# A recurrent attention with an MLP on one core: batch 0's attention in whole chunks of 128 tokens

## The chip, the cores and the metric

One core of a Trainium2 chip runs the kernel. It has a matrix engine (PE, with a weight load, PEld, ahead of each product), three engines for elementwise work (DVE, ACT, POOL), and a queue (SP) that mostly starts DMAs; ACT starts some as well. Each engine takes its own queue in order, and waits where an operand isn't ready. PE and the three others work on SBUF; PE's results go to PSUM banks, which DVE and ACT read.

The metric is the device time of one execution in microseconds (us), as the median of several runs. Before the change that is 420.07 us (three runs, 419.74 to 420.17).

## The reference

Four batches, eight heads, 768 tokens, head dimension 48. The attention keeps a 48x48 state for every batch and head, which decays with w and takes in k times v at each token:

```python
for t in range(S):
    kt, vt, rt = (k[:, :, t], v[:, :, t], r[:, :, t])
    cur = np.einsum('bhd,bhe->bhde', u[None] * kt, vt)
    y[:, :, t] = np.einsum('bhd,bhde->bhe', rt, state + cur)
    state = w[None, :, :, None] * state + np.einsum('bhd,bhe->bhde', kt, vt)
```

The heads side by side give x with 384 columns per token. It is mixed along the tokens through rank 32, and then goes through a two-layer MLP:

```python
xt = x.transpose(0, 2, 1)
h = xt @ U @ V
u = x + h.transpose(0, 2, 1)
ch = np.maximum(u @ w_ch1, 0.0) @ w_ch2
return (u + ch).astype(np.float32)
```

The weights U, V, w_ch1 (384x1536) and w_ch2 (1536x384) come as 64-bit floats, the rest as 32-bit.

## The kernel before

**Attention by chunks.** The loop over tokens is unrolled into chunks of C = 128 tokens, NCH = 6 for a batch. With tables of powers of w, r and k of a chunk are scaled so that the products of r with k, masked to earlier tokens (`am`), times v give the part inside the chunk, and r times the state S gives the part of earlier chunks; the token's own term is `dv` (r times k times u, summed over a head to `dg`, times v). In batch 0 a chunk is done in two halves of 64 tokens: 64x64 scores in four quadrants of the array, one state for each half, and two products that need the odd heads of v with the halves of the rows swapped. That swapped copy, `vsw`, is loaded by DMAs of its own (`a_load_odd`). `a_first` begins chunk 0, `a_part(n, 0)` and `a_part(n, 1)` do the two halves of the output of chunk n and the scores and states of chunk n + 1. Between them a one-element copy (`seen`) makes the second half wait for the first. Of the later batches some chunks use the same functions and others `a_chunk`; the change leaves their computation as it is.

**Preparing a chunk** (`prepare`): `a_load` loads r, k and v; `a_ks` multiplies k by a table (`tab`); `a_tr` turns k and r with four transposes each on PE and scales them on the way out of PSUM to `kT` (ACT or DVE) and `rT` (DVE); `a_dv` and `a_dg` make the token's own term.

**From x to the MLP.** `c_gx` sums U's product with each chunk of x in the bank `wake`, `c_g0` makes `Gs` of it, `c_x` turns x on PE into the banks `pu`, `c_xu` adds V's product with Gs there and splits the result in a high and a low part, `uTh` and `uTl`. The MLP (`m_1`, `m_2`) then needs, for each of 12 slices f, the converted weights `w1s` and `w2s`, and takes three products for each block since high and low parts are multiplied apart. Its first product reads `uTh` of batch 0.

**Weights.** A unit is loaded as 64-bit words (`raw_w`), joined to 32-bit floats by steps on ACT and DVE (names `raw_w`), and split into high and low parts (ACT, then DVE or POOL). At most three units are loaded at a time. Units for slice f are called `raw_w_f`; one is of w_ch1 and one of w_ch2, told apart by their shapes in the DMA queue (128x3x256 and 128x768).

**What sets the order.** `Plan` keeps every operation with a key, a due time given by `at(t, ...)`, and a cost in ns. At build time it schedules them on the five queues by these costs and keys, and the instructions are then issued in the order of the planned starts. So queues mix attention, weights and MLP, and a change of a key or a cost moves instructions on all engines. Where PE would stand idle in the front of the program, the planner adds products of the identity with itself (`wake` with `ident`); they compute nothing that is used. Batches 1 to 3 have their attention in between the MLP products of the batch ahead of them.

## Time and profile before

| | us |
|---|---|
| median of three runs | 420.07 |
| the profiled execution | 420.94 |
| its span, first to last instruction | 419.1 |
| PE busy | 408.1 (97%) |
| DVE busy | 263.9 (63%) |
| ACT busy | 134.8 (32%) |
| POOL busy | 74.6 (18%) |

Busy time of PE counts each product from its start to its modelled end, and products overlap: 97% doesn't say that PE is at its peak, and the wake products are in it. The page's chain of work that ended last lies to 91% on PE, 72% on the MLP's products. The page's row of the sixteen DMA engines, in 40 slices of some 10.5 us, shows them busy through the first half:

```profile
DMA  9978969899557677755677814520100510001001
```

### The profile page before, as it was taken

The numbers are of one execution on the slowest core, as the hardware profiler recorded it, in microseconds if no ns is written. First come the engines' busy times: TensorE is split into PE (matmuls) and PEld (weight loads), VectorE is DVE, ScalarE is ACT, GpSimd is POOL, SyncE is SP. The second block draws the span as 40 slices with busy tenths as digits, with TensorE's granted clock in tenths as the row PEclk, the third lists the DMA queues.
The fourth block names the chain that finished last, engine by engine and source line by source line (L and its number), as shares of the span: only waits on it lengthen the run. The fifth ranks groups of instructions, "written<-read, shape, count | busy, mean of one in ns | idle before, by whom it ended". The sixth has DMA issues, their size and how long they took to land.

```text
span 419.1 us, 12257 instructions
## 1 busy us (share of the span) xinstructions
PE 408.1 (97%) x5164; PEld 393.3 (94%) x5164; DVE 263.9 (63%) x594; ACT 134.8 (32%) x358; POOL 74.6 (18%) x114
## 2 busy tenths in 40 slices
PE   8998999999999999999999999999999999999994
PEld 8887999999999898999999999999999999999993
DVE  6878998889898559877784358866523361122122
ACT  2467967547641415212113130112113121111110
POOL 2642150145621103321000003321000000000000
PEclk9999999999999999999999999999999999999998
DMA  9978969899557677755677814520100510001001
GB/s 145 149 160 256 201 163 242 125 224 234 94 85 154 142 144 132 149 103 87 137 140 107 152 68 64 101 39 2 59 2 0 114 57 2 0 2 58 2 0 61
DMA packets 181951, 43.53 MB, mean 104 GB/s; under 512 B 168961, under 2 KB 180354, under 8 KB 181890
## 3 DMA queue, kind: packets, MB, share of 16 engines
q1 hardware_dynamic: 176706, 41.21, 49.1%
q10 hardware_dynamic: 5184, 1.48, 2.0%
q8 instruction: 42, 0.69, 0.7%
q14 instruction: 19, 0.16, 0.1%
HBM read 36.18 MB, written 6.49 MB: 102 GB/s over the span
## 4 chain that ended last, share of the span: by engine, by line
PE 91%; DVE 4%; ACT 2%; issue 1%; POOL 0%; DVEq 0%; ACTq 0%; POOLq 0%
PE p L347 72%; PE wake L347 3%; PE pav L836 3%; PE pav L842 3%; PE pab L795 3%; PE pab L810 2%; PE pu L347 2%; PE ptk L756 1%; PE pG L1040 1%; PE pav L821 1%; DVE am L967 1%; PE ptr L756 1%; ACT dv L725 1%; DVE SW L1004 1%; DVE ut L1136 1%
## 5 line engine op out<-in xcount | busy, mean ns | idle before, releaser
L347 PE MATMUL p<-uTh,w1s 128*128 128x384 f32 x576 | 147.5, 336 | 0.0
L1163 DVE SCALAR_TENSOR_TENSOR hl<-p,hh 128x384 fp32r<-128x384 f32 x96 | 53.2, 555 | 114.9 <-ACT hh L1162 114.5
L347 PE MATMUL p<-w2s,hh 128*128 128x384 f32 x576 | 119.9, 340 | 0.5 <-ACT hh L1162 0.4
L1162 ACT ACTIVATE hh<-p 128x384 fp32r<-128x384 f32 x96 | 47.2, 491 | 222.8 <-PE p L347 220.2
L347 PEld LDWEIGHTS p<-uTh,w1s 128*128 128x128 f32 x576 | 103.2, 188 | 0.5
L347 PEld LDWEIGHTS p<-w2s,hh 128*128 128x128 f32 x576 | 100.0, 188 | 2.4 <-ACT hh L1162 1.1
L347 PE MATMUL p<-uTl,w1s 128*128 128x384 f32 x288 | 96.5, 335 | 0.0
L347 PE MATMUL p<-w2s,hl 128*128 128x384 f32 x288 | 66.1, 335 | 0.0
L347 PEld LDWEIGHTS p<-uTl,w1s 128*128 128x128 f32 x288 | 54.0, 188 | 0.3 <-DVE uTl L1095 0.3
L347 PEld LDWEIGHTS p<-w2s,hl 128*128 128x128 f32 x288 | 51.4, 188 | 0.1
L795 PE MATMUL pab<-rT,kT 48*64 48x64 f32 x768 | 30.6, 223 | 1.8 <-issue 1.0
L836 PE MATMUL pav<-vsw,am 64*64 64x48 f32 x384 | 30.4, 222 | 0.1
L842 PE MATMUL pav<-S,rT 48*64 48x48 f32 x704 | 29.5, 218 | 0.0
L836 PEld LDWEIGHTS pav<-vsw,am 64*64 64x64 f32 x384 | 25.2, 134 | 1.9 <-issue 1.0
L795 PEld LDWEIGHTS pab<-rT,kT 48*64 48x64 f32 x768 | 24.9, 134 | 2.1 <-ACT dv L725 0.8
L842 PEld LDWEIGHTS pav<-S,rT 48*64 48x64 f32 x704 | 25.8, 135 | 0.0
L836 PE MATMUL pav<-ldv,am 64*64 64x48 f32 x320 | 24.2, 221 | 0.0
L705 POOL MEMSET ks<- 128x128 f32 x24 | 4.9, 204 | 101.9 <-PE pav L842 57.0
L967 DVE TENSOR_TENSOR am<-pab,mask 128x256 f32<-128x256 f32 x48 | 19.4, 417 | 5.4 <-PE pab L810 3.9
L836 PEld LDWEIGHTS pav<-ldv,am 64*64 64x64 f32 x320 | 20.2, 134 | 2.5 <-issue 2.1
L810 PE MATMUL pab<-ldv,ks 64*48 64x48 f32 (+1 forms) x576 | 21.1, 212 | 0.0
L995 DVE TENSOR_TENSOR S<-pab,SW 112x192 f32<-112x192 f32 x40 | 14.0, 351 | 8.2 <-PE pab L810 5.5
(136 smaller groups left out, 520.2 us busy)
## 6 DMA issues: line engine op xcount, KB each, us to landing
raw_w<-in_moe_w_ch_dram SPq DMA_DIRECT2D x24, 384.0 KB, 4.7
out_dram<-x SPq DMA_DIRECT2D x21, 192.0 KB, 2.4
ldr<-in_r_dram SPq DMA_DIRECT2D x20, 192.0 KB, 3.1
ldk<-in_k_dram SPq DMA_DIRECT2D x20, 192.0 KB, 3.5
ldv<-in_v_dram SPq DMA_DIRECT2D x20, 192.0 KB, 3.9
bl<-in_r_dram SPq DMA_DIRECT2D x79, 48.0 KB, 2.6
bl<-in_k_dram SPq DMA_DIRECT2D x79, 48.0 KB, 2.4
vsw<-in_v_dram SPq DMA_DIRECT2D x42, 48.0 KB, 2.7
```

The source lines that it names most:

```text
L347: return nc.tensor.matmul(*args, **kw)
L705: op("POOL", 250, lambda: nc.gpsimd.memset(ks.t[:, :, D:], 0.0), [(ks, "pad")], [])
L725: nc.scalar.activation(dv.t[:, h], vt()[:, h], AF.Copy, scale=dg.t[:, h:h + 1])
L756: nc.tensor.transpose(pt.t[:, q * C:(q + 1) * C], src().rearrange("p h d -> p (h d)")[:, q * PE_:(q + 1) * PE_], ident_)
L795: return [lambda q=q, i=i: nc.tensor.matmul(pt.t[(i ^ j) * C2:(i ^ j) * C2 + C2, q * C2:(q + 1) * C2], lhsT=kT.t[rows, q, i * C2:(i + 1) * ...
L810: return nc.tensor.matmul(pt.t[j * HP:j * HP + m, SU + q * D:SU + (q + 1) * D], lhsT=ks.t[half, 2 * q + j, :m], rhs=vt()[half, 2 * q + j, ...
L836: return nc.tensor.matmul(to(q, j, i), lhsT=am[j].t[half, q, :], rhs=vsw[n].t[half, q, :] if j else vt()[half, 2 * q, :], start=((i == 1 i ...
L842: return nc.tensor.matmul(to(q, row, i), lhsT=rT.t[rows, q, i * C2:(i + 1) * C2], rhs=St[n, i].t[rows, q, :], start=False, stop=((alone or ...
L967: on_dve(256, lambda e: e.tensor_tensor(am.t, abs_[n][j].t[:, :SU].rearrange("p (h t) -> p h t", h=NP), mask_.unsqueeze(1).broadcast_to([1 ...
L995: on_dve(192, lambda e, new=new, ptv=ptv, dec=decayed[n, j]: e.tensor_tensor(new.t, ptv(), dec.t, ALU.add), [new], [pt, decayed[n, j]])
L1162: on_act(384, lambda: nc.scalar.activation(hh.t, pt.t[:, :TB], AF.Relu), [hh], [pt])
L1163: on_dve(384, lambda e: e.scalar_tensor_tensor(hl.t, pt.t[:, :TB], 0.0, f32(hh.t), ALU.max, ALU.subtract), [hl], [pt, hh])
```

## The change

Batch 0 gets functions of its own. A chunk is now taken whole: `f_scores` makes 128x128 scores, heads of even number in the upper half of the array's rows and odd ones in the lower (head dimension 48 on 64 rows each), and masks them with a 128x128 mask `before`; `f_state` makes one state for each chunk with full 128-row products; `f_out` makes the part inside the chunk (`inner`, all 128 rows) and that of the state (`outer`, the two row halves), into two banks, one for even and one for odd heads, and adds dv in two halves of 192 columns. No swapped copy of v is loaded for batch 0, and `seen` goes from it.

The powers of w come from doubling (`powers`): w is loaded as four rows of 112 and turned on PE, then each of seven products on DVE doubles the number of powers, up to 128; a reversed copy of them, turned on PE, is the table `tabf` for batch 0. The tables of the later batches are made from the same powers further down (`tables`, `turn_table`). ks is on POOL from chunk 2 on, dv on POOL for all chunks of batch 0, and the zeroing of pads moves from DVE to POOL.

U is kept once instead of three times, and batch 0 sums its product with x in four groups of 32 columns (`g_sum`), in the way of the later batches; `c_g` replaces `c_g0`, so Gs comes by four copies to `gf` and three steps on it.

Keys and costs of the planner change: batch 0's chunks are due every 4.5 instead of 5.5, the MLP's begin at 42 instead of 46. The planner now starts engines at times of their own, holds back a ready operation for a more urgent one that is about to be ready, and adds a wake product only where more of a gap is left.

```diff
+    KS = 2
+    NQA = 3
...
-    tabT = cbuf([PD, 2, NP, C2 + 2], F32, "tabT")
+    tabT = cbuf([PD, NP, C2], F32, "tabT")
     wi = cbuf([PD, NP, 1], F32, "wi")
     wm = cbuf([PD, NP, 1], F32, "wm")
+    wif = cbuf([PD, NP, 1], F32, "wif")
+    wmf = cbuf([PD, NP, 1], F32, "wmf")
...
-    Uf = cbuf([128, NCH, 3, R], F32, "Uf")
+    Uf = cbuf([128, NCH, 1, R], F32, "Uf")
...
+    pw = big([PD, NP, C + 2], F32, "pw")
+    tabf = big([128, DM], F32, "tabf")
...
+    def powers():
+        p = pw.t
+        op("POOL", 112, lambda: nc.gpsimd.memset(p[:, :, 0:1], 1.0), [(pw, 0)], [])
+        pt0 = bank("tr", "pt_w")
+        pe(120, lambda: nc.tensor.transpose(pt0.t[:PD, :NP], wq.t, ident_[:NP, :NP]), [pt0], [wq])
+        on_dve(4, lambda e: e.tensor_scalar(p[:, :, 1:2], pt0.t[:PD, :NP].unsqueeze(2), W_LO, W_HI, ALU.max, ALU.min),
+               [(pw, 1)], [pt0])
+        m = 1
+        while m < C:
+            on_dve(4 * m, lambda e, m=m: e.tensor_mul(p[:, :, m + 1:2 * m + 1], p[:, :, 1:m + 1],
+                                                      p[:, :, m:m + 1].broadcast_to([PD, NP, m])), [(pw, 1)], [])
+            m *= 2
+        back = xbuf([PD, NP, C], F32, "hh", NH, "back")
+        on_dve(512, lambda e: e.tensor_copy(back.t, p[:, :, C - 1::-1]), [back], [pw])
+        turn_table(back, tabf, "tabf")
+        on_dve(4, lambda e: e.reciprocal(wif.t, p[:, :, C:C + 1]), [wif], [pw])
+        on_dve(4, lambda e: e.tensor_copy(wmf.t, p[:, :, C:C + 1]), [wmf], [pw])
...
-        if n < 4 or not front(n):
+        if not front(n):
...
+                  kb + [tabf if front(n) else tab],
+                  only="DVE" if n < KS else "POOL" if front(n) else None)
...
+        if i == 0 and front(n):
+            on_dve(512, lambda e: e.tensor_tensor(xT.t[:PD], by_pair(), pw.t[:, :, :C], ALU.mult), [xT], [pt, pw])
+            return
...
+    def f_scores(n):
+        rT, kT = trs[n]
+        abs_[n] = [bank(t, f"pab_{n}_{j}") for j, t in enumerate(AB)]
+        def product(q, j):
+            rows = head_rows(j)
+            return nc.tensor.matmul(abs_[n][j].t[:, q * C:(q + 1) * C], lhsT=kT.t[rows, q, :], rhs=rT.t[rows, q, :],
+                                    start=True, stop=True)
+        pe(950, lambda: in_turn(*([lambda q=q, j=j: product(q, j) for q in range(NP)] for j in range(2))), abs_[n], [rT, kT],
+           tiled=True)
+        ams[n] = []
+        for j in range(2):
+            am = xbuf([128, NP, C], F32, "bl", 5, f"am_{n}_{j}")
+            ams[n].append(am)
+            on_dve(512, lambda e, am=am, j=j: e.tensor_tensor(am.t, abs_[n][j].t.rearrange("p (q t) -> p q t", q=NP),
+                                                              before_.unsqueeze(1).broadcast_to([128, NP, C]), ALU.mult),
...
+        def product(q, j):
+            m = D if j else HP
+            return nc.tensor.matmul(pt.t[j * HP:j * HP + m, q * D:(q + 1) * D], lhsT=ks.t[:, 2 * q + j, :m],
+                                    rhs=vt()[:, 2 * q + j, :], start=True, stop=True)
+        pe(480, lambda: in_turn(*([lambda q=q, j=j: product(q, j) for q in range(NP)] for j in range(2))), [pt], [ks, *vb],
+           tiled=True)
...
+    def f_out(n):
+        vt, vb = vs[n]
+        rT = trs[n][0]
+        avp[n] = [bank(t, f"pav_{n}_{j}") for j, t in enumerate(("av", "mm"))]
+        def inner(q, j, i):
+            return nc.tensor.matmul(avp[n][j].t[i * C2:(i + 1) * C2, q * D:(q + 1) * D],
+                                    lhsT=ams[n][j].t[:, q, i * C2:(i + 1) * C2], rhs=vt()[:, 2 * q + j, :],
+                                    start=(q == 0), stop=(not n and q == NP - 1), skip_group_check=True)
+        def outer(q, j):
+            rows = head_rows(j)
+            return nc.tensor.matmul(avp[n][j].t[:, q * D:(q + 1) * D], lhsT=rT.t[rows, q, :], rhs=St[n, 0].t[rows, q, :],
+                                    start=False, stop=(q == NP - 1), skip_group_check=True)
+        for j in range(2):
+            pe(500, lambda j=j: in_turn(*([lambda q=q, i=i: inner(q, j, i) for q in range(NP)] for i in range(2))),
+               [avp[n][j]], [ams[n][j], *vb], tiled=True)
+        if n:
+            pe(950, lambda: in_turn(*([lambda q=q, j=j: outer(q, j) for q in range(NP)] for j in range(2))), avp[n], [rT, St[n, 0]],
+               tiled=True)
+        x = xs[n] = xbuf([128, DM], F32, "x", NX, f"x_{n}")
...
+    def g_sum(pt, c0, ns):
+        w4 = DM // 4
+        for n in ns:
+            for g in range(4):
+                nc.tensor.matmul(pt.t[g * R:(g + 1) * R, c0:c0 + w4], lhsT=Uf.t[:, n % NCH, 0],
+                                 rhs=xs[n].t[:, g * w4:(g + 1) * w4],
+                                 start=(c0 == 0 and n % NCH == 0), stop=(n % NCH == NCH - 1), skip_group_check=True)
+    def c_gx(*ns):
+        return pe(170 * len(ns), lambda: g_sum(wk, 128, ns), [(wk, "g")], [Uf] + [xs[n] for n in ns], tiled=True)
...
-    T0, PER = 46.0, 1.95
+    T0, PER = 42.0, 1.85
+    UV, GX, UVC = -84.9, (3, 33.0), (30.0, 33.0)
     EARLY, LEAD = 4, 12.0
-    FRONT, EACH = 9.0, 5.5
+    FRONT, EACH = 9.0, 4.5
+    UB = -88.5
+    SC, SU_, TABLES = 2.0, 0.0, 30.0
...
+        for i, f in enumerate([fs[j] for j in (2, 0, 1, 3)] if front(n) else fs):
...
+            if front(n):
+                at(t - SC, lambda n=n: f_scores(n))
+                at(t - SU_, lambda n=n: f_state(n))
+                at(t, lambda n=n: f_out(n))
+                at(t - 0.1, lambda n=n: a_dg(n))
+                if c >= GX[0]:
+                    at(max(t + per - 0.05, GX[1] + 0.1 * c), lambda n=n: gx.append(c_gx(*(range(n + 1) if n == GX[0] else [n]))))
+                continue
```

**PE, inside batch 0.** Before, at the change from chunk 2 to chunk 3: the end of a half (products with S and with ks), the transposes of r, wake products, and the next half, in which results (`pav`) alternate with the next chunk's scores (`pab`):

```order
L842 MATMUL pav_424<-S_0_334,rT_290 64x48
L810 MATMUL pab_1_482<-ld_98,ks_265 48x48
L756 MATMUL ptr_524<-ident,ld_106 128x128 x4
L347 MATMUL wake<-ident 128x128 x5
L836 MATMUL pav_552<-vsw_182,am_1_529 64x48
L795 MATMUL pab_0_554<-rT_546,kT_514 64x64
L836 MATMUL pav_552<-ld_98,am_0_478 64x48
```

Now, from the scores of chunk 3 to its output; rows that only repeat (scores, state products and outer products alternate between the two head groups) are left out:

```order
L965 MATMUL pab_0_469<-rT_415,kT_412 128x128
L965 MATMUL pab_1_471<-rT_415,kT_412 128x128
L778 MATMUL ptr_487<-ident,ldr_232 128x128 x4
L778 MATMUL ptk_504<-ident,ks_442 128x128 x4
L987 MATMUL psu_516<-ld_179,ks_341 64x48
L987 MATMUL psu_516<-ld_179,ks_341 48x48
L1015 MATMUL pav_0_527<-ld_179,am_0_490 64x48 x8
L1015 MATMUL pav_1_545<-ld_179,am_1_511 64x48 x8
L1021 MATMUL pav_0_527<-S_429,rT_415 128x48
L1021 MATMUL pav_1_545<-S_429,rT_415 128x48
```

Scores of a chunk stand together, then the transposes of the next chunk, the state products (`psu`), the inner products, eight for each group of heads, and the outer ones; the wake products between them are gone.

**DVE, at the end of batch 0's attention.** Before, from the state of chunk 5's first half on: masks `am`, first steps on the raw weights, V's split, and the result x of chunk 4:

```order
L995 TENSOR_TENSOR S_0_871<-pab_0_825,SW_0_805 112x192
L967 TENSOR_TENSOR am_0_878<-pab_0_825,mask 128x256
L540 TENSOR_SCALAR raw_w_0_779<-raw_w_0_779 128x384
L540 TENSOR_SCALAR raw_w_0_786<-raw_w_0_786 128x384
L605 TENSOR_TENSOR V_886<-pv_875,V_886 32x384
L475 TENSOR_SCALAR wrc<-wrow 1x384
L605 TENSOR_TENSOR V_886<-pv_883,V_886 32x384
L967 TENSOR_TENSOR am_1_929<-pab_1_894,mask 128x256
L974 TENSOR_TENSOR x_936<-pav_823,dv_633 128x384
```

Now, from x of chunk 4 to x of chunk 5 (raw_w_0_485, raw_w_1_514 and raw_w_2_614 are units of w_ch1; raw_w_2_614 is the fifth unit in the DMA queue):

```order
L1034 TENSOR_TENSOR x_685<-pav_0_633,dv_392 128x4x48
L1034 TENSOR_TENSOR x_685<-pav_1_648,dv_392 128x4x48
L573 SCALAR_TENSOR_TENSOR raw_w_0_485<-raw_w_0_485 128x384
L566 TENSOR_SCALAR raw_w_2_614<-raw_w_2_614 128x384
L576 SCALAR_TENSOR_TENSOR raw_w_0_485<-raw_w_0_485 128x384
L973 TENSOR_TENSOR am_0_710<-pab_0_688,before 128x512
L973 TENSOR_TENSOR am_1_719<-pab_1_690,before 128x512
L631 TENSOR_TENSOR V_717<-pv_707,V_717 32x384
L573 SCALAR_TENSOR_TENSOR raw_w_1_514<-raw_w_1_514 128x384
L631 TENSOR_TENSOR V_717<-pv_714,V_717 32x384
L576 SCALAR_TENSOR_TENSOR raw_w_1_514<-raw_w_1_514 128x384
L1034 TENSOR_TENSOR x_777<-pav_0_723,dv_483 128x4x48
```

Chunk 5's two masks now stand behind a step on raw_w_2_614, and its x behind the split of V and two more steps on a raw weight.

**SP, the loads.** Before, the first loads after w; ld_89, ld_95 and ld_98 hold chunks 0, 1 and 2:

```order
L659 DMA ld_89<-in_r_dram 128x8x48
L659 DMA ld_89<-in_v_dram 128x8x48
L421 DMA ub<-in_u_dram 128x384
L659 DMA ld_95<-in_r_dram 128x8x48
L659 DMA ld_95<-in_v_dram 128x8x48
L659 DMA ld_98<-in_r_dram 128x8x48
```

Now the same place, with chunks 0, 1 and 2 in ld_91, ld_104 and ld_109:

```order
L682 DMA ld_91<-in_r_dram 128x8x48
L682 DMA ld_91<-in_v_dram 128x8x48
L682 DMA ld_104<-in_r_dram 128x8x48
L682 DMA ld_104<-in_v_dram 128x8x48
L440 DMA ub<-in_u_dram 128x384
L682 DMA ld_109<-in_r_dram 128x8x48
```

The broadcast of u (`ub`) has moved behind the loads of chunk 1. Further down, before, from the last load of chunk 5 to the first weight (raw_u and raw_v are U and V):

```order
L659 DMA ldv_590<-in_v_dram 128x8x48
L519 DMA raw_u<-in_moe_U_dram 128x6x64
L519 DMA raw_v<-in_moe_V_dram 32x384 x4
L671 DMA vsw_722<-in_v_dram 64x4x48 x2
L519 DMA raw_w_0_779<-in_moe_w_ch_dram 128x3x256
```

Now, from the same load on:

```order
L682 DMA ldv_383<-in_v_dram 128x8x48
L545 DMA raw_u<-in_moe_U_dram 128x6x64
L545 DMA raw_v<-in_moe_V_dram 32x384 x4
L545 DMA raw_w_0_485<-in_moe_w_ch_dram 128x3x256
L545 DMA raw_w_0_502<-in_moe_w_ch_dram 128x768
```

The swapped copies `vsw` ahead of the first weight are gone, as are four more in SP's queue and six in ACT's.

More of the change, by code (lines that the diff above doesn't have):

```diff
@@ L56 @@
     LANDS = 1650
-    CROWD, CROWDED = 1.29, 32000
+    BEGINS = {"DVE": 900, "ACT": 800, "PE": 1650, "POOL": 1000, "SP": 800}
+    SPARE = 0.15
+    CROWD, CROWDED = 1.2, 32000
+    HOLD, HELD = 3, 50000
     DRAINS = 200
@@ L94, in op @@
                 o.allocs.append(b)
-                ring = self.rings.setdefault(b.tag, {"order": [], "next": 0, "free": [(0.0, "")] * b.bufs, "last": None})
+                ring = self.rings.setdefault(b.tag, {"order": [], "next": 0, "free": [(-99.0, "")] * b.bufs, "last": None})
                 ring["order"].append(b)
@@ L218, in schedule @@
                         continue
+                    while e != "SP" and t < self.HELD:
+                        held = [(u, p, k) for u, p, k in at if p.key[0] < o.key[0] - self.HOLD and len(p.ways) == 1 and u > t + 1
+                                and 2 * (u - t) < o.ways[i][1] - self.OVERLAP[e] - 60]
+                        if not held:
+                            break
+                        t, o, i = min(held, key=lambda a: a[0])
                     if best is None or t < best[0]:
@@ L460, in tables @@
-        on_dve(4, lambda e: e.tensor_mul(wi.t, top(1), top(1)), [wi], [sq])
-        pt = bank("tr", "pt_tab")
-        def turn():
-            for q in range(NP):
-                nc.tensor.transpose(pt.t[:, q * PE_:q * PE_ + PD], tw.t[:, q, :], ident_[:PD, :PD])
-        pe(900, turn, [pt], [tw])
-        on_act(384, lambda: nc.scalar.copy(tab.t.rearrange("p (h d) -> p h d", d=D),
-                                           pt.t.rearrange("p (h d) -> p h d", d=HP)[:, :, :D]), [tab], [pt])
+        p = pw.t
@@ L712, in a_dv @@
                        wbuf([128, H, D], F32, "dv", 2, f"dv_{n}"))
-        on_either(384, lambda e: e.tensor_mul(dv.t, rt()[:, :, :D], kt()[:, :, :D]), [dv], rb + kb,
-                  only="POOL" if front(n) and n else None)
-        on_either(384, lambda e: e.tensor_mul(dv.t, dv.t, ub.t), [dv], [ub], only="POOL" if front(n) and n else None)
+        for a_, b_, w_, r_ in ((rt, kt, [dv], rb + kb), (lambda: dv.t, lambda: ub.t, [dv], [ub])):
+            on_either(384, lambda e, a_=a_, b_=b_: e.tensor_mul(dv.t, a_()[:, :, :D], b_()[:, :, :D]), w_, r_,
+                      only="POOL" if front(n) else None)
     def a_dg(n):
@@ L725, in small @@
                 nc.scalar.activation(dv.t[:, h], vt()[:, h], AF.Copy, scale=dg.t[:, h:h + 1])
-        if front(n):
-            for h in range(0, H, 2):
-                op("ACT", 560, lambda h=h: small(h, h + 2), [(dv, h)], vb + [dg])
-            return
         one_of([("ACT", 1900, small, False),
@@ L921, in a_part @@
         else:
[L922 removed]
+            pe(950 if last else 1000, second, wr, rd + [seens[n]], tiled=True)
         if nxt:
@@ L1009, in a_st @@
             op("POOL", pool(192), lambda one=one: one(nc.gpsimd), [dec], [new, wm], lock=True,
-               alt=[("DVE", dve(192), lambda one=one: one(nc.vector), True), ("ACT", NP * (act(D) - 94) + 94, four, False)])
+               alt=([] if front(n) else [("DVE", dve(192), lambda one=one: one(nc.vector), True)]) +
+               [("ACT", NP * (act(D) - 94) + 94, four, False)])
     decayed = {}
```

194 lines of the change are left out of this document (100 added, 94 removed).

## The prediction

> **What bounds the kernel now.** I read the stretches of the span first: start and end, length, then busy us (instructions) of PE, PEld, DVE, ACT and POOL, the granted clock, the DMA share and GB/s.
>
> ```profile
> 0.00:52.39 52.39, 47.99 (x973) 44.12 (x974) 41.83 (x113) 32.83 (x107) 18.47 (x39) 1.00 0.93 182
> 52.39:413.17 360.78, 360.12 (x4192) 349.21 (x4191) 221.57 (x481) 101.96 (x253) 56.17 (x76) 1.00 0.46 92
> 413.17:419.10 5.93, 0.00 (x0) 0.00 (x0) 0.56 (x2) 0.00 (x0) 0.00 (x0) 0.69 0.31 105
> ```
>
> The cuts are the start of the first product of the MLP and the end of the last one. Between them PE has one wait worth a row, in the list of PE's waits for that stretch (in all, times, longest):
>
> ```profile
> PE p L347 <- ACT hh L1162: 0.4, 1, 0.4
> ```
>
> So the span is P + 360.8 + 5.9, where P is the start of the first MLP product, 52.39 now. By the order lists, PE's instructions from that product on are the same before and after, kind by kind and in number. The change can only move P, or put new waits into the 360.8 us.
>
> What sets P is the stretch ahead of it. Rows of its chain of waits (start, length, engine and output):
>
> ```profile
> 1.66 4.45 PE wake L347 x20
> ...
> 6.54 1.56 PE wake L347 x14
> ...
> 12.07 0.62 PE pab L795 x32
> ...
> 25.38 0.27 DVE S L995
> 25.64 0.46 DVE x L974
> 26.11 0.60 DVE rT L765
> 26.71 0.47 DVE dg L721
> ...
> 27.20 1.02 ACT dv L725 x4
> ...
> 29.77 0.59 PE ptk L756 x4
> 30.35 0.45 PE ptr L756 x4
> ...
> 42.30 0.44 DVE am L967
> ```
>
> No engine bounds it alone: DVE, the fullest beside PE, has 41.83 us in 52.39, and PE's 47.99 hold the wake products that fill its waits. The chain passes from engine to engine, twice for every chunk: scores on PE, mask and state on DVE, result on PE. The first scores are at 12.07, the last mask at 42.30: 30 us for six chunks.
>
> **The change, part by part.** I went down the four queues in the new order, row by row, with durations of this trace.
>
> Tables. The old chain ran from the squares to the copy of tab:
>
> ```profile
> 4.98 0.97 DVE L441 TENSOR_TENSOR sq<-sq 112x4 f32<-112x4 f32 x5
> ```
>
> ```profile
> 10.08 0.48 ACT L467 COPY tab<-pt_tab 128x384 f32<-128x384 f32 x1 [6.15 <-PE pt_tab L465]
> ```
>
> The new one is a transpose, the clamp and seven doublings (0.19 each while small, as the squares, up to 0.4 for 256 columns; 1.8 in all), a reversed copy of 512 columns (0.7), four transposes (0.6) and the copy on ACT (0.5): 3.6 us against 5.6. That gain is hidden, since u's broadcast load ub now comes last:
>
> ```profile
> 9.68 1.01 POOL L715 TENSOR_TENSOR dv<-dv,ub 128x384 f32<-128x384 f32 x1 [7.32 <-DMA ub<-in_u_dram]
> ```
>
> ub landed at 9.7 us. It now stands behind two more loads of 192 KB, 1.1 us each at the 182 GB/s of the stretch, and behind less of vsw: about 11.7. In the DVE order the reduction dg of chunk 0 stands ahead of chunk 0's masks, so these start at 11.7 + 1.0 (POOL) + 0.5 (dg) = 13.2.
>
> Pace of a chunk. DVE: two masks of 512 columns (0.60 each, as rT), rT 0.60, S 0.27, dg 0.47, two halves of x (0.27 each, as S): 3.1 us. PE: transposes 0.59 + 0.45. The new products aren't in the trace. Scores, state, two inner groups and the outer one are eight products each, 16 records. From below a record takes 19 ns (32 in 0.62), so 0.31 us a group; from above 56 ns (eight in 0.45 for four 128x128 transposes), so 0.90. Scores and outer products load 128 columns as the transposes do: 0.90. State and inner products load at most 64: 0.45. PE's sum is 1.04 + 0.90 + 0.45 + 0.90 + 0.90 = 4.2 us, at the lower ends 2.6. I take 4.2. The TensorEngine Tiling (Array Packing) page of the Trainium skill (section Key Properties) says that different tiles load weights and multiply in parallel; by it scores would be 0.45 and the sum 3.75 a chunk, which no run here shows and which leaves the forecast, since P is set by the weights.
>
> The other two engines (start, length, group, and the idle time before it; then a group with its mean ns):
>
> ```profile
> 30.45 1.14 ACT L771 ACTIVATE kT<-ptk,wi 112x128 f32<-112x128 f32 x4 [0.85 <-PE ptk L756]
> ```
>
> ```profile
> L713 POOL TENSOR_TENSOR dv<-ld 128x384 f32<-128x384 f32 x3 | 3.0, 1001 | 0.2 <-DMA ld<-in_k_dram 0.2
> ```
>
> ACT: dv 2.04 (eight), kT 1.14, SW 1.0 (four, as dv): 4.2 at most, and the order gives one dv to DVE and two SW to POOL. POOL: ks and two products of dv, 3.0 us. None is above 4.2 us, so chunk 5's masks could start at 13.2 + 5 x 4.2 = 34.2, against 42.30 for the last one now.
>
> The weights. In the new DVE order a step on the fifth weight unit, raw_w_2_614, stands ahead of chunk 5's two masks, and a queue runs in order. So its landing matters:
>
> ```profile
> 16.71 3.04 SPq L671 DMA_DIRECT2D vsw<-in_v_dram  x4
> ...
> 29.00 1.88 SPq L671 DMA_DIRECT2D vsw<-in_v_dram  x2
> 30.92 1.62 SPq L519 DMA_DIRECT2D raw_w<-in_moe_w_ch_dram  x3
> ...
> 35.84 0.79 SPq L519 DMA_DIRECT2D raw_w<-in_moe_w_ch_dram  x1
> ```
>
> ```profile
> raw_w<-in_moe_w_ch_dram SPq DMA_DIRECT2D x1, 384.0 KB, 4.6
> ```
>
> The second fence gives the landing time of the issue at 35.84: it lands at 40.4, 9.5 us after the first weight's issue at 30.92. The copies vsw leave the front. By SP's own time that is 3.04 + 1.88 = 4.9 us, and the first weight goes out at 26.0; by bytes, twelve copies of 48 KB at 182 GB/s, it is 3.2 us, and 27.7. I take 26.5, nearer SP's rows. The fifth unit then lands at 36.0, later than 34.2: it decides.
>
> From there I count between starts: 0.47 for a step of 384 columns on DVE (dg, above), 0.44 on ACT (first fence). The end of the chain is read from batch 1, whose steps the new batch 0 takes (second fence); the third is the copies to uTh:
>
> ```profile
> 41.44 0.56 ACT L566 ACTIVATE raw_w<-raw_w 128x384 f32<-128x384 f32 x1
> 41.88 0.54 ACT L544 ACTIVATE raw_w<-raw_w 128x384 int32<-128x384 uint8 x1
> ```
>
> ```profile
> 143.37 0.24 ACT gf L1047
> ...
> 145.68 0.76 PE pu L347 x3
> ```
>
> ```profile
> 51.54 2.37 ACT L1094 CAST uTh<-pu 128x384 fp32r<-128x384 f32 x6
> ```
>
> DVE: from 36.0, that step and the next 0.8, masks 1.2, four steps of V and weights 1.9, two halves of x 0.5: chunk 5's x is ready at 40.4. ACT has nine conversions between unit 0's joined word (36.8) and gf: 36.8 + 0.5 + 9 x 0.44 = 41.3, later than x and its products on PE (40.4 + 0.4). From gf to pu 2.3 (143.37 to 145.68), from there to uTh 0.45 (an estimate: 0.76 for three such products, the first of them and its way to ACT), one uTh 0.45: P = 44.5. The old Gs took two steps where the new path takes gf and then Gs; that is in this sum.
>
> So P falls by 52.39 - 44.5 = 7.9 us. The profiled execution took 420.94 us, 1.84 around its span, and would take 413.0; the median of the runs shown lies 0.87 lower, at 420.07, so **412.2 us**.
>
> The 360.8 us. At P the new order has about three and a half weight units converted, the old five. That is 1.5 units of three steps of 0.47, 2.1 us, which DVE owes at the start of the MLP, where it has none free:
>
> ```profile
> 52.40:60.00 7.60, 7.60 (x43) 7.30 (x43) 7.60 (x16) 5.63 (x18) 4.84 (x6) 1.00 0.51 86
> ```
>
> Going down the queues, the closest use is the fourth w1 unit, ready about 1 us before PE wants it. I count nothing, with 0 to 2.1 as bounds.
>
> **The rivals.**
>
> Weights early enough. If they come 2 us before my 36.0 or conversions wait less, the attention decides: 34.2 + masks 1.3 + inner 0.45 + outer 0.9 + x 0.7, then 0.4 + 2.3 + 0.9 and half a us of conversions in between: P = 41.7, 409.4 us. For it: vsw leaves ACT's queue too, which I counted by bytes alone. Against it: so many conversions ahead of x and gf. Chance 0.15.
>
> Weights no earlier. If the loads of r, k and v, not the copies, fill the queue until 30.9, then P = 44.5 + 4.4 = 48.9, 416.6 us. Against it: the 4.9 us of SP's rows. Chance 0.14.
>
> Debt in the MLP. P as forecast, but DVE's 2.1 us come out as PE's waits: 414.3 us. Chance 0.10.
>
> Slower. The wake products on the identity go from 56 to 11, all of these ahead of the tables. If PE then runs at the rate of the first wakes (20 records in 4.45 us, 0.22 each, against 14 in 1.56, 0.11 each), a chunk costs 8.4 us on PE: masks of chunk 5 at 13.2 + 42.0 = 55.2, P near 63, 431 us. It turns to a loss above 6.4 us a chunk, (52.39 - 13.2 - 7.0) / 5, where 7.0 is the way from these masks to P. The TensorE: Matmul & The Clock Gate page of the Trainium skill (section What's actually happening) has this rule: half rate by default, and again after some 3.4 us of idleness; the first twenty wakes agree. Against it: PE's work of 2.6 to 4.2 us in 4.2 leaves no long gap. The granted clock, 1.00 even in the stretch of the slow wakes, doesn't tell it; the spacing does. Chance 0.04.
>
> No change that counts, if attention's gain and the weights' are both lost: 0.02.
>
> **How the numbers follow.** The forecast has 0.55; with its own spread it reaches from 411 to 413.5. Both neighbours, 409.4 and 416.6, are likely enough to be held: the range is 409.2 to 416.7. Left out are the slow clock, no change, and the tails. Faster by over 0.2% (0.84 us, about what a measurement here can tell from no change): 0.55 + 0.15 + 0.14 + 0.10 = 0.94; within it 0.02; slower 0.04.
>
> **What would show it.** The first product with uTh at 44 to 45. The first weight's issue near 26.5, the step on the fifth unit waiting for its DMA, and chunk 5's masks right behind it, at 36 to 37. Transposes from chunk 1 on at 0.11 each. PE idle after P under 1 us. If chunk 5's masks wait for PE instead, the pace was wrong; if P is right and the end isn't, the MLP got new waits.

## The result and the profile after

The changed kernel took 414.37 us (median of four runs, 414.0 to 414.7), the kernel before 420.12 (four runs, 419.74 to 422.01): ratio 0.986, interval 0.984 to 0.988. It is 5.75 us faster; 7.9 were forecast. The profiled execution took 414.39 us, 1.69 around its span of 412.7.

The stretches of the span after, cut as those of before (first product with uTh, last product; same columns):

```profile
0.00:44.21 44.21, 39.54 (x610) 35.03 (x610) 37.01 (x84) 29.18 (x96) 24.42 (x50) 1.00 0.88 196
44.21:405.96 361.75, 360.36 (x4193) 349.00 (x4192) 227.70 (x484) 99.93 (x246) 63.64 (x86) 1.00 0.47 93
405.96:412.70 6.74, 0.00 (x0) 0.00 (x0) 0.56 (x2) 0.00 (x0) 0.00 (x0) 0.71 0.27 95
```

P is 44.21 against a forecast of 44.5: 8.18 us came off the front. The middle is 0.97 us longer than the 360.78 of before, and what lies behind the last product 0.81. In the middle PE was idle for 1.39 us, 0.66 before; the other 0.24 of the 0.97 is busy time and has no name. The list of PE's waits from P on has one worth naming (total, times, longest), where that of before had 0.4 for hh:

```profile
PE p L359 <- DVE uTl L1198: 0.8, 1, 0.8
```

The front's chain of waits after (start, length, engine and output):

```profile
11.83 1.16 PE pab L965 x16
...
24.38 0.96 PE pab L965 x16
25.34 0.58 PE ptr L778 x4
25.93 0.44 PE ptk L778 x4
26.36 0.54 PE psu L987 x13
...
26.96 0.93 PE pav L1015 x31
27.89 1.03 PE pav L1021 x16
28.92 0.96 PE pab L965 x16
...
34.57 0.27 DVE raw_w L566
34.84 0.47 DVE raw_w L576
35.31 1.20 DVE am L973 x2
...
41.38 0.52 ACT Gs L1156
...
42.51 1.03 DVE raw_w L573 x2
43.53 1.30 DVE raw_w L576
44.84 0.03 issue
44.87 0.57 DVE uTl L1198
```

Before, this chain went from engine to engine within every chunk. Now it stays on PE from 11.83 to 33.5: a chunk every 4.5 us (24.38 to 28.92), and no step of it is another engine's. From 34 us on it runs through conversions of weights on DVE and ACT. The step at 34.57 is the fifth weight unit's, which I had taken for the one that decides; it waits for no load. The first weight goes out much earlier than I forecast (SP's queue; start, length, line, kind, tiles, count), and u's load lands earlier, at 10.60, where its landing ends POOL's wait:

```profile
23.32 9.13 SPq L545 DMA_DIRECT2D raw_w<-in_moe_w_ch_dram  x8
```

```profile
10.60 2.39 POOL L740 TENSOR_TENSOR dv<-dv,ub 128x384 f32<-128x384 f32 x2 [1.30 <-DMA ub<-in_u_dram]
```

Chunk 0's masks, before (a row of the chain) and after (DVE's timeline):

```profile
13.22 0.74 DVE am L967 x2
```

```profile
13.02 1.29 DVE L973 TENSOR_TENSOR am<-pab,before 128x512 f32<-128x512 f32 x2 [0.19 <-PE pab L965]
```

They start 0.20 us earlier, so nearly all of the 8.18 is made behind them. No run takes back the whole chunks alone; how much of it is theirs and how much is that of the earlier loads stays open.

### The profile page after: what moved, and what is told of

It is laid out like the page before. It is cut to its first block, busy times and chain, and to the rows that moved or that the text cites. A ratio compares the mean times of both kernels' runs of the same rounds, so it can differ in the third digit from the quotient of the medians.

```text
span 412.7 us, 11498 instructions
## 1 busy us (share of the span) xinstructions
PE 399.9 (97%) x4801; PEld 384.0 (93%) x4801; DVE 265.3 (64%) x568; ACT 129.1 (31%) x341; POOL 88.1 (21%) x135
## 4 chain that ended last, share of the span: by engine, by line
PE 91%; DVE 5%; ACT 1%; issue 1%; POOL 0%; DVEq 0%; POOLq 0%
PE p L359 73%; PE pav L862 2%; PE pav L868 2%; PE pab L821 2%; PE pab L836 2%; PE pab L965 1%; PE pav L1015 1%; PE pav L1021 1%; PE ptr L778 1%; PE pG L1129 1%; PE ptk L778 1%; PE pav L847 1%; PE psu L987 1%; DVE pw L477 1%; PE wake L359 1%; DVE raw_w L576 1%
## 5 line engine op out<-in xcount | busy, mean ns | idle before, releaser
L821 PE MATMUL pab<-rT,kT 48*64 48x64 f32 x576 | 22.8, 224 | 0.0
L868 PE MATMUL pav<-S,rT 48*64 48x48 f32 x528 | 21.8, 219 | 0.0
L862 PE MATMUL pav<-vsw,am 64*64 64x48 f32 x288 | 21.6, 221 | 0.0
L862 PE MATMUL pav<-ldv,am 64*64 64x48 f32 x288 | 21.6, 221 | 0.0
L821 PEld LDWEIGHTS pab<-rT,kT 48*64 48x64 f32 x576 | 18.6, 135 | 0.7 <-issue 0.7
L862 PEld LDWEIGHTS pav<-vsw,am 64*64 64x64 f32 x288 | 18.3, 134 | 1.0 <-issue 1.0
L1101 DVE TENSOR_TENSOR S<-pab,SW 112x192 f32<-112x192 f32 x30 | 10.5, 350 | 13.4 <-PE pab L836 11.3
L862 PEld LDWEIGHTS pav<-ldv,am 64*64 64x64 f32 x288 | 18.1, 134 | 1.0 <-issue 0.7
L868 PEld LDWEIGHTS pav<-S,rT 48*64 48x64 f32 x528 | 18.9, 135 | 0.0
L1305 DVE TENSOR_TENSOR x<-p,x 128x384 f32<-128x384 f32 x30 | 14.9, 548 | 4.6 <-PE p L359 4.4
```

Source lines behind the costliest of these rows:

```text
L821: return [lambda q=q, i=i: nc.tensor.matmul(pt.t[(i ^ j) * C2:(i ^ j) * C2 + C2, q * C2:(q + 1) * C2], lhsT=kT.t[rows, q, i * C2:(i + 1) * ...
L862: return nc.tensor.matmul(to(q, j, i), lhsT=am[j].t[half, q, :], rhs=vsw[n].t[half, q, :] if j else vt()[half, 2 * q, :], start=((i == 1 i ...
L868: return nc.tensor.matmul(to(q, row, i), lhsT=rT.t[rows, q, i * C2:(i + 1) * C2], rhs=St[n, i].t[rows, q, :], start=False, stop=((alone or ...
L1101: on_dve(192, lambda e, new=new, ptv=ptv, dec=decayed[n, j]: e.tensor_tensor(new.t, ptv(), dec.t, ALU.add), [new], [pt, decayed[n, j]])
L1305: on_dve(384, lambda e, x=x, pt=pt: e.tensor_tensor(x.t, pt.t[:, :DM], x.t, ALU.add), [x], [pt])
```

## The experiments

Each kernel is the changed one with the edit shown. "P" is the start of the first product with uTh, "middle" the time from there to the last product, both from the one profiled execution; "clock" is the mean granted TensorE clock of all its executions. The runs of before beside them lay at 420.0 to 420.5 in the median, with a clock of 0.996 to 1.000.

| run | chunk 5's masks | P | middle | time, us (n) | clock |
|---|---|---|---|---|---|
| changed | 35.22 | 44.21 | 361.75 | 414.37 (4) | 0.994–0.999 |
| e1 low first | 40.57 | 49.55 | 363.30 | 415.44 (5) | 0.980 twice, 0.995–0.998 |
| e2 no outer | 34.33 | 43.24 | 361.45 | 412.52 (1) | 0.998 |
| e3 copies back | 40.69 | 49.66 | 361.40 | 418.10 (1) | 0.988 |
| e4 slow tables | 42.73 | 51.70 | 361.42 | 420.75 (1) | 0.979 |
| e5 changed again | 34.91 | 43.89 | 361.40 | 413.62 (5) | 0.991–0.998 |
| e6 wakes | 34.95 | 43.93 | 361.44 | 413.28 (5) | 0.996–0.999 |
| e7 order | 34.89 | 43.88 | 362.47 | 414.39 (4) | 0.995–0.999 |
| e8 rows apart | 45.33 | 55.47 | 361.46 | 425.01 (1) | 0.975 |
| e9 no outer, short dg | 32.97 | 41.91 | 361.42 | 411.42 (1) | 0.998 |
| e10 slow tables, wakes | 38.88 | 47.86 | 361.45 | 417.73 (5) | 0.995–0.999 |
| e11 slow tables again | 44.84 | 53.82 | 362.01 | 421.63 (10) | 0.976–0.996 |
| e12 low later | 35.33 | 44.32 | 361.73 | 413.71 (5) | 0.997–0.998 |

The changed kernel took 414.37 in one series and 413.62 in another (e5), with 420.12 and 420.49 for the kernel before: differences under 0.8 us between series say nothing. e5 to e8 are one series, e1 to e4 another, e9 to e12 a third.

### What sets the pace of the chunks: e2 and e9

e2 leaves out the outer products, e9 shortens dg as well:

```diff
-            pe(950, lambda: in_turn(*([lambda q=q, j=j: outer(q, j) for q in range(NP)] for j in range(2))), avp[n], [rT, St[n, 0]],
+            pe(950, lambda: None, avp[n], [rT, St[n, 0]],
```

```diff
-        on_dve(384, lambda e: e.tensor_reduce(dg.t, dv.t, AX.X, ALU.add), [dg], [dv])
+        on_dve(384, lambda e: e.tensor_reduce(dg.t, dv.t[:, :, :1] if front(n) else dv.t, AX.X, ALU.add), [dg], [dv])
```

> The 40 outer products of batch 0 (16 records, 1.0 us, for each of chunks 1 to 5) are left out; every engine's order is otherwise that of the changed kernel, and the part of the result that comes from the state is missing. Theory A (PE's own work sets the pace of the chunks): four outer groups stand ahead of chunk 5's masks, so these start 3 to 4 us earlier than 35.22, the scores come every 3.5 us instead of 4.5, until another engine binds; the first product with uTh falls from 44.21 to 40 to 41.5. Theory B (the forecast's: the fifth weight unit's step ahead of chunk 5's masks decides): the masks stay within 0.7 us of 35.22 whatever PE does, with VectorE waiting for that unit's load, and the first product with uTh falls by 1 us at most, the last outer group.

> The outer products are left out, as in the second experiment, and VectorE's sum dg of batch 0 goes over one column of 48 instead of all (0.54 us down to about 0.17 for each chunk); both parts of the result are missing. There the 4.1 us taken from PE had moved chunk 5's masks by 0.9 us only. Theory A (VectorE's queue is as full as PE's, and set the pace as soon as PE was lighter: it was busy 18.55 of 20 us from 15 to 35): with six dg shorter by 0.37 the masks start 1.2 to 2.2 us earlier again, at 32.1 to 33.1, and the first product with uTh comes at 41.0 to 42.2. Theory B (the pace is then set by ScalarE or by the loads of U and of the weights): the masks stay at 33.8 to 34.5, and the first product with uTh at 42.7 to 43.4.

In e2 there are 4.1 us less on PE ahead of chunk 5's masks, and these come 0.9 us earlier. My theory A of that run, that PE alone sets the pace, fell by its numbers. B's bound for P was met and that for the masks missed by 0.2, and its reason isn't there: no step on a weight waits for a load. What took over is in DVE's timeline of e2 (start, length, line, operation, tiles, and in brackets idle time and its releaser):

```profile
20.66 1.27 DVE L973 TENSOR_TENSOR am<-pab,before 128x512 f32<-128x512 f32 x2
21.86 0.68 DVE L787 TENSOR_TENSOR rT<-ptr,pw 112x512 f32<-112x512 f32 x1
22.45 0.34 DVE L996 TENSOR_TENSOR S<-psu,SW 112x192 f32<-112x192 f32 x1
22.72 1.00 DVE L747 TENSOR_REDUCE dg<-dv 128x8 f32<-128x384 f32 x2
23.64 0.61 DVE L1034 TENSOR_TENSOR x<-pav,dv 128x192 f32<-128x192 f32 x2
24.17 1.27 DVE L973 TENSOR_TENSOR am<-pab,before 128x512 f32<-128x512 f32 x2
```

In this stretch, from mask to mask, there is no bracket: DVE doesn't wait. PE does, in the same kernel:

```profile
35.06 1.27 PE L1015 MATMUL pav<-ldv,am 128*64 128x48 f32 x32 [0.62 <-DVE am L973]
```

So e9 asks whether it is DVE. Six dg shorter by 0.37 are 2.2 us; masks and P came 1.36 and 1.33 us earlier again, inside A's bounds and outside B's. PE and DVE are both nearly full in the front: from 15 to 35 us PE is busy for 20.00 us of 20 in the changed kernel and DVE for 18.55; taking work from one hands the pace to the other. ACT isn't far behind: it is busy for 18.75 in that stretch of e9, and PE's longest wait inside e2's chunks, 0.73 at 27.31, is for kT on ACT.

### Where the weights stand: e3

```diff
+                for m in range(NCH if i == 2 and n == NCH - 1 else 0):
+                    t = work.tile([128, NP, D], F32, tag="vsw", name=f"copy_{m}", bufs=3)
+                    for g in range(2):
+                        q.dma_start(t[(1 - g) * C2:(2 - g) * C2], v[0, 1::2, m * C + g * C2:m * C + (g + 1) * C2, :].rearrange("h p d -> p h d"))
```

> Twelve loads of 48 KB of v, which nobody reads, go out on SP's queue behind chunk 5's loads and ahead of U, V and the weights, as many bytes as the copies that the change took away; all else is in the order of the changed kernel. By bytes at the stretch's 200 GB/s it is 2.9 us, by SP's rows of before (0.76 to 0.94 for each) 9 to 11 us: the first weight's issue goes from 23.3 to 26 at least, to 33 at most. Theory A (weights had slack in the changed kernel: the step on the fifth unit at 34.49 waited for no load): a delay of 3 us is absorbed but for 1 us or less, and the first product with uTh stays under 45.5; a delay of 9 us moves it by about the delay less the slack, to 48 to 50. Theory B (weights decide, as forecast): it moves by the whole delay, 47 at least, and the step on the fifth unit waits for its DMA.

SP's queue and three of DVE's steps in e3 (the last one is the step on the fifth unit):

```profile
18.84 8.95 SPq L687 DMA_DIRECT2D copy<-in_v_dram  x12
...
31.38 8.90 SPq L545 DMA_DIRECT2D raw_w<-in_moe_w_ch_dram  x8
```

```profile
32.13 0.36 DVE L573 SCALAR_TENSOR_TENSOR raw_u<-raw_u 128x192 int32<-128x192 int32 x1 [2.90 <-ACT raw_u L592]
...
36.86 0.36 DVE L566 TENSOR_SCALAR raw_w<-raw_w 128x384 int32<-128x384 uint8 x1 [1.77 <-DMA raw_w<-in_moe_w_ch_dram]
...
39.95 0.36 DVE L566 TENSOR_SCALAR raw_w<-raw_w 128x384 int32<-128x384 uint8 x1 [0.39 <-DMA raw_w<-in_moe_w_ch_dram]
```

Twelve loads of 48 KB took 8.95 us of the queue, 0.75 each: SP's rows priced them right, the bytes (2.9 us) did not. With the weights as late as before the change (31.4 against 30.9), conversions of U and of a weight block DVE in front of chunk 4's and chunk 5's masks, and P goes to 49.66. The step on the fifth unit waits for its DMA here, by 0.39, and chunk 5's masks follow at 40.69: with weights as late as that, the forecast's mechanism is there. P = 49.66 lies within the bounds of both theories. It also holds a stretch of half clock that begins at 34.7, behind the wait at 32.13, so the pure price of the delay is not measured. The slack of the changed kernel lies between 0 and these 8 us; e3 doesn't narrow it.

### The tables: e4 and e10

```diff
+            def double(e, m=m):
+                for _ in range(6 if m == C2 else 1):
+                    e.tensor_mul(p[:, :, m + 1:2 * m + 1], p[:, :, 1:m + 1], p[:, :, m:m + 1].broadcast_to([PD, NP, m]))
+            on_dve(4 * m, double, [(pw, 1)], [])
```

e10 has in addition 18 and 7 wake products in PE's queue ahead of the transposes of the tables and of ks:

```diff
+        for o, m in zip(plan.turns, (18, 7)):
+            plan.woken.extend((o.start - 1, fill) for _ in range(m))
```

> The last doubling on VectorE, 256 columns, is made six times instead of once: 5 x 0.4 = 2.0 us longer, the length that the old chain of tables had over the new one; nothing else changes. Theory A (the tables are on the path: chunk 0's scores end at 12.99, after dg at 12.83): chunk 0's masks go from 13.02 to about 15.0, and since PE sets the pace from there the first product with uTh goes from 44.21 to about 46.2 and the time to 416.4. Theory B (the forecast's: u's load hides the tables): the masks move by 0.5 us at most, the time by less.

> The last doubling six times, as before, with 18 more wake products ahead of the tables' transposes and 7 ahead of the first of ks, so that PE's gaps of 4.16 and 1.70 us are filled. Theory A (PE's gap brought the granted clock of 0.50 from 9.4 to 22.6 us): all executions keep a mean clock of 0.99 or more; what remains is the length of the tables, 2.9 us by that trace (5.53 against 2.67), so the first product with uTh comes at 46.8 to 47.8 and the time is 416.5 to 417.5. Theory B (tables hidden behind u's load): at full clock it comes at 44.0 to 44.7, 414 to 415 us. Theory C (the half clock isn't from the gap): mean clocks near 0.980 and 420 us come here too.

In e4 the clock fell (below), so that P = 51.70 says nothing of the tables. e10 keeps it. Chunk 0's masks wait for its scores there, at

```profile
16.68 1.29 DVE L979 TENSOR_TENSOR am<-pab,before 128x512 f32<-128x512 f32 x2 [0.19 <-PE pab L971]
```

3.66 us after the changed kernel's 13.02, and P follows by 3.65. The doublings are 3.0 us longer (5.67 against 2.67), and the wakes end 0.7 us after the copy that they were to bridge. What the tables grew by, with this 0.7, comes out in the end: theory B, that u's load hides them, falls. A's mechanism held; P and the median, 47.86 and 417.73, lie just above its bounds of 47.8 and 417.5.

### The half clock: e1, e4, e8, then e5, e6, e11

e1's own question is below; its trace showed something else. Windows of e1 (stretch, length, busy us of PE, PEld, DVE, ACT and POOL with counts, granted clock, DMA share, GB/s), and one of the changed kernel:

```profile
8.00:9.70 1.70, 1.00 (x8) 0.76 (x8) 1.67 (x6) 0.48 (x1) 1.10 (x2) 0.98 0.83 147
9.70:23.30 13.60, 13.24 (x127) 11.32 (x127) 8.44 (x17) 5.98 (x24) 6.84 (x10) 0.50 1.07 184
23.30:30.00 6.70, 6.70 (x139) 6.30 (x138) 5.33 (x12) 3.33 (x14) 6.05 (x9) 1.00 0.93 306
```

```profile
9.70:23.30 13.60, 12.95 (x238) 11.28 (x238) 13.11 (x26) 7.90 (x32) 11.42 (x16) 1.00 0.97 184
```

PE's order is the same in both up to there. At a granted clock of 0.50, e1's PE does 127 instructions where the changed kernel does 238, and P comes at 49.55. What precedes it are two gaps of PE, 1.10 and 1.06 us in e1, that the change has opened. The first fence has them in the changed kernel, the second has the gap of e4, which belongs to what follows:

```profile
7.95 0.60 PE L462 MATMUL pt_tabf<-ident,back 112*128 112x112 f32 x4 [1.17 <-DVE back L481]
...
10.25 0.63 PE L778 MATMUL ptk<-ident,ks 128*128 128x128 f32 x4 [1.26 <-DVE ks L731]
```

```profile
10.81 1.01 PE L462 MATMUL pt_tabf<-ident,back 112*128 112x112 f32 x4 [4.16 <-DVE back L483]
```

e5 is the changed kernel unaltered. e6 adds five wake products ahead of each of these two; e11 is e4 again, in more executions.

```diff
+        for o in plan.turns[:2]:
+            plan.woken.extend((o.start - 1, fill) for _ in range(5))
```

> The changed kernel itself, unaltered, in more runs on this chip. In the run before, a kernel whose PE queue is this one's up to 40 us had a granted clock of 0.50 from 9.7 to 23.3 us in two executions of five (mean clock 0.980, span 5 to 6 us longer) and 0.99 or more in the others; kernel before had 0.997 in all of seven. Theory A (the two gaps that the change opens in PE's front, 6.8 to 7.9 and 9.0 to 10.2 us, bring it, at an edge that chance decides): some executions here too show a mean clock near 0.980 and a time of 419 to 421, the others 414 to 415. Theory B (it was the edit of that kernel): all executions show 0.994 or more, as the first four of the changed kernel did, and 414 to 415.

> The changed kernel with ten more wake products on the identity, five ahead of the tables' four transposes and five ahead of the first transposes of ks, where PE waited 1.17 and 1.26 us; nothing else. Theory A (the gaps bring the half clock): no execution falls below a mean clock of 0.99, all come at 414 to 415, and the front starts no later than 0.3 us after the changed kernel's. Theory B (the half clock has another cause): the low mean clock of 0.980 with 419 to 421 us comes as often as without them.

> The kernel with the slow tables and no added wakes, unaltered, in more executions on the same chip. Theory A (a gap of 4 us in PE's early queue brings the half clock): every execution, or all but one, shows a mean clock near 0.980 and 420 to 421.5 us. Theory B (chance, apart from the gap): most executions show 0.995 and 416.5 to 417.5 us.

In e4's and e11's profiles the gap ahead of the tables is 4.16 and 3.84 us long, and the clock falls in both. With these long gaps 9 of 11 executions (e4 and e11) had a mean clock under 0.99; with the same tables and the gaps filled (e10) none of 5 had, at 417.0 to 417.8 instead of 418.4 to 423.6. That the gap brings it is shown there, as a chance: e11's theory A wanted all executions but one near 0.980, and five of ten were above 0.985; its theory B fell as well. The mean clock isn't the whole of it: two of e11's executions at 0.996 took 419.4, some 2 us more than e10's at 0.995 and more, and why is open. With the short gaps of the changed kernel it is rarer. Counting every kernel whose PE queue is the changed one's up to there, the mean clock was 0.980 or less in two of e1's five executions and in e8's one; e2, e3 and e9 kept the full clock at that place, and the changed kernel's own nine executions had none as low (0.991 at least). The length doesn't tell it: gaps of 0.99 and 1.08 lost the clock in e8, 1.42 and 1.07 kept it in e5. e6, e7 and e12, which fill the short gaps, had none in 14. For the short gaps that is too few to prove the cause or the cure; e5's theory A predicted some, and there was none. e6 is level with e5 (413.28 and 413.62).

The TensorE: Matmul & The Clock Gate page of the Trainium skill (section What's actually happening) gives half clock after an idle window of about 3.4 us and full clock after one busy window. The gap of e4, 4.16 us, is long enough for that, though the clock fell 2.6 us into it (at 9.2). The gaps of 0.99 to 1.99 us in e1, e3 and e8 are shorter, and the clock fell after them too. The return doesn't agree: in e1 PE was busy 13.24 of 13.60 us and stayed at 0.50 for all of them.

### The 0.8 us at the MLP's start: e1, e7, e12

e1 puts the conversion steps that stand on DVE between Gs and the first uTl behind the third uTl. e7 has that and e6's wakes, and on ACT puts one conversion step behind the third uTh and two behind the first hh. e12 puts the second tile's three uTl behind the first hl as well. The edit is made in the finished order; `later` moves an operation, and what depends on it, back to a time:

```diff
+        first, third = self.lows[0].start, self.lows[2].start
+        late = [o for o in self.signs if first - 2200 < o.start < third]
+        for i, o in enumerate(sorted(late, key=lambda o: o.start)):
+            o.start = third + 1 + i
```

```diff
+        high, third = m["hh"].start, m["uh"].start
+        late = sorted((o for o in plan.ops if o.eng == "ACT" and o.fn in plan.casts and third - 1600 < o.start < high), key=lambda o: o.start)
+        for i, o in enumerate(late):
+            later(o, (third if o.start < third else high) + 1 + i)
```

```diff
+        for i, o in enumerate(plan.lows[3:6]):
+            later(o, m["hl"].start + 1 + i)
```

> The three conversion steps that stand on VectorE between Gs and the first uTl go behind the first tile's third uTl; nothing else moves. Theory A (queue order cost the 0.8 us): in the changed kernel the first uTl starts at 44.87, behind steps of 1.03 and 1.39 us, although its uTh is ready at about 44.0; here it starts at 43.9 to 44.2, PE's wait for uTl (0.8) goes, the stretch from the first product with uTh to the last product falls from 361.75 to about 361.0, and the time from 414.4 to about 413.6. Rival B (the three steps are owed anyway): a later weight comes late by up to 1.4 us, PE waits for it instead, and the time stays at 414.4. Rival C (it is POOL, at work from 43.08 to 45.69 beside them, that slows whatever step DVE runs there): uTl itself takes over 1 us, and the wait shrinks by half at most.

> The ten wake products, the three VectorE steps behind the third uTl as in the first experiment, and on ScalarE one conversion step behind the third uTh and two behind the first hh. Theory A (the debt of conversions was paid at whichever hand-over stood behind it in a queue: first uTl, then hh, and uses of the weights come later): PE's waits of 0.8 for uTl and of 0.7 for hh are both gone, the first uTh comes 0.3 to 0.4 earlier, no new wait over 0.3 follows, the stretch from the first product with uTh to the last is 361.0 or less, and the time is 412.8 to 413.6. Rival B (conversions are owed at any order): PE waits for a weight or for the next hh by 0.5 to 1.0 us, and the time stays at 414 to 415.

> The reordered kernel of the run before, and the second tile's three uTl on VectorE, which PE wants only 60 us later, behind the first hl. There the wait for uTl had gone and one of 0.9 for the first hl had come in its place, since hl stood behind these three and a conversion step. Theory A (urgent steps stood behind steps that can wait): hl comes before PE wants it, PE has no wait over 0.3 in the first 10 us of the MLP, the stretch from the first product with uTh to the last is 361.0 or less, and the time is 412.3 to 413.2. Rival B (VectorE is full there, and a wait of 0.5 to 1.0 us returns at the next hl or weight): 413.6 to 414.6.

PE's waits from P on, of e1, of e7 and of e12:

```profile
PE p L364 <- ACT hh L1270: 0.7, 1, 0.7
...
PE p L364 <- DVE x L1310: 0.3, 1, 0.3
```

```profile
PE p L368 <- DVE hl L1283: 0.9, 1, 0.9
PE p L368 <- DVE x L1322: 0.4, 1, 0.4
```

```profile
PE p L368 <- DVE x L1323: 0.3, 1, 0.3
PE p L368 <- DVE w1s L623: 0.3, 1, 0.3
```

The wait for uTl goes each time, and each time another comes: for the first hh, for the first hl, for a weight. The middle is 363.3, 362.5 and 361.7, where the unaltered order had 361.40 to 361.75, and e7 took 414.39 beside e6's 413.28. Rival B held for the time in e7 and e12: no order tried made the kernel faster. e12 has what A wanted of the first 10 us, no wait over 0.3, and still neither the middle nor the time that A named. Rival C of e1 fell: the first three uTl took 1.48 us together, with POOL at work beside them. A likely reason is in the windows of the MLP's first 35.7 us, before and after (columns as above):

```profile
52.39:68.07 15.68, 15.68 (x90) 15.38 (x90) 14.47 (x31) 9.88 (x27) 6.25 (x8) 1.00 0.82 190
68.07:88.07 20.00, 20.00 (x279) 19.24 (x278) 17.75 (x39) 11.40 (x25) 3.26 (x6) 1.00 0.94 195
```

```profile
44.21:59.89 15.68, 14.92 (x86) 14.60 (x86) 14.98 (x30) 10.04 (x28) 6.89 (x8) 1.00 0.86 205
59.89:79.89 20.00, 20.00 (x189) 19.13 (x190) 18.99 (x40) 13.32 (x32) 3.97 (x6) 1.00 0.81 189
```

DVE works 33.97 us there (14.98 + 18.99), 1.75 more than before (14.47 + 17.75), with 1.71 left of 35.68. No run took conversions away from DVE, so the rest is argued from these rows.

### Row halves in turn or apart: e8

```diff
-        pe(950, lambda: in_turn(*([lambda q=q, j=j: product(q, j) for q in range(NP)] for j in range(2))), abs_[n], [rT, kT],
+        pe(950, lambda: in_turn([lambda q=q, j=j: product(q, j) for j in range(2) for q in range(NP)]), abs_[n], [rT, kT],
```

and the same for the outer products.

> Scores, state part and their like in batch 0: the scores and the outer products are issued first for all heads of the array's upper row half and then for all of the lower, four and four, instead of in turn; the same products otherwise. Theory A (products in different row halves overlapped little: eight took 0.96 to 1.03 us in the changed kernel, not the 0.90 of whole-array transposes that I put in the sum, let alone half of it): eight still take 1.0 to 1.2 us. Theory B (they overlap in turn): eight in a row in one half take markedly longer, 1.5 us or more, each chunk grows by 1 us, and the first product with uTh comes 3 to 5 us later.

Outer products and scores of the changed kernel, then scores and outer products of e8, at full clock (PE's timeline):

```profile
27.82 1.10 PE L1021 MATMUL pav<-S,rT 48*128 48x48 f32 x16
28.75 1.13 PE L965 MATMUL pab<-rT,kT 48*128 48x128 f32 x16
```

```profile
44.14 1.71 PE L965 MATMUL pab<-rT,kT 48*128 48x128 f32 x16
...
48.37 1.58 PE L1021 MATMUL pav<-S,rT 48*128 48x48 f32 x16
```

Four and four, a group takes 1.6 to 1.7 us, in turn 1.1: the halves overlap, for about a third of the time. Theory B held for the group. Chunks grew less than it said, 0.6 us (a chunk every 5.16 us from 27.6 us on); the first records of the scores there alternate with the last outer products (32.74 to 33.18), which would explain it. P = 55.47 holds a half clock and can't be read.

## Why the prediction was right, and where it was off

**P, forecast 44.5, was 44.21 (43.89 in e5).** The size was right, and the reason for it was not; that the number came out is luck. I had the fifth weight unit decide, with the masks right behind its load at 36 to 37. In fact the first weight went out at 23.32, not 26.5, the step on the fifth unit waited for nothing, and the masks came at 35.22 after PE and DVE. That is the mechanism of the rival "Weights early enough", whose masks, at 34.2, were 1.0 early and whose way from there to P, 7.5 us, was 1.5 short. The step that failed is the weights' new time, "I take 26.5", with 26.0 as the earliest. I had the copies' own rows right (4.9 us; e3's twelve cost 0.75 each) and left out that the loads ahead of them could move as well: chunk 3's went out at 8.32 instead of 11.74, 3.4 us earlier, of which SP kept 2.7 until the weights.

**Pace, forecast 4.2, was 4.5.** PE's terms were each a little short: scores 0.96 and outer 1.03 for 0.90 each, state 0.54 plus a piece for 0.45, inner 0.97 for 0.90. The larger error was DVE, 3.1 us in my sum: it left out dv, kT and ks of the first chunks and the conversions in front of the last masks. e2 and e9 show DVE nearly as full as PE. The 3.75 a chunk that I worked out by the TensorEngine Tiling (Array Packing) page of the Trainium skill (section Key Properties) halved the scores alone, though the outer products use two row halves as well: with both it is 3.3. The trace has 4.5, with 0.96 for the scores against 0.45; e8 shows that tiles do overlap, by a third and not by half.

**Tables, "3.6 us, and that gain is hidden".** They took 4.6 (pw's clamp at 4.49, tabf's copy done at 9.07), and were not hidden. u's load landed at 10.6, not 11.7; dg was done at 12.83 and the scores at 12.99, so both ends met at the 13.02 that I forecast as 13.2. e10 shows that tables are on the path: longer ones would have cost, which I counted at nothing. Against the kernel before, the first masks still moved by 0.20 us only.

**From the masks to P, forecast 7.7, was 9.0.** Two conversion steps of V and two of weights stood ahead of x, as said; uTh then stood behind two conversions on ACT, from 42.45 to 43.48, and began at 43.50, 0.88 after the start of pu at 42.62 instead of 0.45. The masks were 1.6 us earlier than forecast (36.8) and this was 1.3 longer; the two errors nearly cancelled in P.

**The 360.8 us, counted at nothing, "with 0 to 2.1 as bounds", was 361.75.** This is the term that was mis-sized: 0.97. The debt of conversions was named, and priced at zero because its closest use looked ready 1 us early. Its first creditor was not a weight but uTl, behind conversions in the same queue, and in e1 and e7 hh and hl. The rival "debt in the MLP" had the mechanism; 2.1 us was its upper end, and 0.6 to 1.0 came out. That these are the debt is argued: of the 0.97, 0.73 is idle time of PE, and no run has fewer conversions.

**The rest of the 2.2 us between 412.2 and 414.37.** Behind the last product lay 6.74 us, not 5.93; in the twelve other profiles it was between 5.3 and 6.5, so that 0.8 is scatter that no experiment here explains. And I took 0.87 off for the profiled execution against the median, which this time was at the median. Together: -0.29 + 0.97 + 0.81 + 0.85 - 0.15 (1.69 around the span for 1.84) = 2.19.

**The slow rival.** Its mechanism exists: after gaps in PE's early work the chunks can run at half rate. Two things in it were wrong. The granted clock does tell it (0.50 in e1). And the full rate returned after 13.5 us there, so that P came at 49.55 and not at 63. The changed kernel's own nine executions were spared; the chance of 0.04 was for all of the loss in the usual run, and what the runs show is a smaller loss in some executions of e1 and in e8's.

## What to carry to other kernels

When a chain of waits passes from engine to engine, add up the whole queue of each engine over the stretch, conversions and helpers included, before naming a bound: here 4.1 us less on PE moved the masks by 0.9, because DVE was nearly as full. A front that ends earlier starts the next stage with less of its side work done; if an engine is nearly full there, the rest can come out as a wait, and here reordering only picked the place. Products that look idle may hold the clock: look at PE's gaps, not only at the work, before taking them away, and run it often enough to see the rare case.
